# Sixty tiny matmuls at the head of the TensorE program, a reordered weight cast, a load in halves and an uneven last output

## The chip, the cores and the metric

The kernel runs on one core of one Trainium2 chip. The metric is the device time in microseconds (us). Each run also lists the core's span, which is 1.7 us shorter than its time in every run here (229.38 and 227.7 us in the first profile, for instance). Spans are used below where single executions are compared. A profile is the record of one such execution.

Engines: PE is TensorE, PEld its weight loads, DVE VectorE, ACT ScalarE, POOL GpSimd, SPq and ACTq the queues on which SyncE and ScalarE issue DMAs.

## The reference, cut to what matters

Linear attention with decay for 4 batches, 8 heads, 768 tokens of 64, followed by a gated feed-forward block (FFN) on 3072 tokens of 512:

```python
intra = einsum('bhic,bhjc->bhij', q, k) * Dmask      # per block, Dmask = lam ** (i - j), causal
inter = einsum('bhid,bhde->bhie', q * lam_pow, kv_state)
out   = einsum('bhij,bhjd->bhid', intra, v) + inter
kv_state = lam_block * kv_state + einsum('bhsd,bhse->bhde', k * rev_pow, v)
...
x = out as (3072, 512)
g = x @ w_gate
result = (g * sigmoid(g) * (x @ w_val)) @ w_out
```

Everything that decays comes from `lam`, eight numbers. They are spread over the partitions by one small matmul, the "lambda matmul" below.

## The kernel before

The kernel casts all inputs to bf16 and works on groups of 256 tokens. PE does everything in program order: attention of the first two groups, then FFN steps with the attention of later groups between them. Before its data arrives, PE is given filler matmuls whose results nobody reads:

```python
lam_ps = bank()
warm_up(4)                                   # four fillers of 512 columns (L130)
nc.tensor.matmul(lam_ps[:, 0:H], ones[:, 0:128], lam_row, ...)   # the lambda matmul (L163)
warm_up(3)
...
nc.scalar.activation(ln_lam, lam_ps[:, 0:H], AF.Ln)              # all decay tables follow (L175)
```

Further fillers stand between the attention matmuls of the first two groups (`warm_into`, L167). The plan of the FFN steps, where the change moves lines (steps between the lines shown are left out):

```python
at(s0[4], load_group, 2, "v")                # one DMA of 512 KB
at(s0[8], v_scale, 2, nc.gpsimd)             # v * decay for 8 heads in one instruction (L238)
...
at(s1b[3], cast_scaled, 5)                   # casts of group 5, then its DMA transpose (L251)
at(s1b[4], wo_cast)                          # output-weight casts (L232), 12 steps in six pieces
at(s1b[4], wo_cast)
at(s1b[6], wo_cast)
at(s1b[6], wo_cast)
at(s1b[6], v_scale, 5, nc.gpsimd)
at(s1b[8], wo_cast)                          # the fifth piece
at(s1b[10], wo_cast, ACTC)                   # the sixth, on ScalarE
at(s1b[11], ffn_out, 0, 0)                   # first output tile (L547): needs all six
at(s1b[11], ahead, 5)                        # group 5: update (L382: needs its v scale), scores (L326)
```

and the last output tile, which leaves in two parts:

```python
halves = ((0, DM // 2, nc.scalar.copy, nc.scalar), (DM // 2, DM, nc.vector.tensor_copy, nc.sync)) if last else ...
```

Of the kernel before, what the change touches and what calls it, by code (L numbers as in the profile page):

```python
# [19 lines left out]
@with_exitstack  # L20
def kernel(
    ctx: ExitStack,
    tc: tile.TileContext,
    q: bass.AP,
    k: bass.AP,
    v: bass.AP,
    lam: bass.AP,
    moe_w_gate: bass.AP,
    moe_w_val: bass.AP,
    moe_w_out: bass.AP,  # L30
    out: bass.AP,
):
    nc = tc.nc
    with tc.manual_schedule():
        _body(ctx, tc, nc, q, k, v, lam, moe_w_gate, moe_w_val, moe_w_out, out)


def _body(ctx, tc, nc, q, k, v, lam, moe_w_gate, moe_w_val, moe_w_out, out):
    B, H, S, D = q.shape
# [3 lines left out]
    DM = H * D  # L43
# [35 lines left out]
    def bank():  # L79
        b = banks[ring[0] % 8]  # L80
        ring[0] += 1
        return b
# [41 lines left out]
    warm = nc.const_aps.tensor(1.0, [128, 512], BF16)  # L124
    ones = const.tile([1, 128], FP32, name="ones")
    nc.vector.memset(ones, 1.0)
    def warm_up(n, cols=512):
        b = bank()
        for _ in range(n):
            nc.tensor.matmul(b[:, 0:cols], warm[:, 0:128], warm[:, 0:cols], start=True, stop=True)  # L130
# [28 lines left out]
           for b in range(B)]  # L159

    lam_ps = bank()
    warm_up(4)
    nc.tensor.matmul(lam_ps[:, 0:H], ones[:, 0:128], lam_row, start=True, stop=True)  # L163
    warm_up(3)
# [373 lines left out]
    def ffn_out(t, b, last=False):  # L538
        h_sb = st[("h", t)]
        osb = osb_pool.tile([128, DM], FP32, name="osb", tag="osb")  # L540
        row = groups[2 * t + b // 2][0] * S + (groups[2 * t + b // 2][1] * 2 + b % 2) * BLK
        halves = ((0, DM // 2, nc.scalar.copy, nc.scalar), (DM // 2, DM, nc.vector.tensor_copy, nc.sync)) \
            if last else ((0, DM, nc.scalar.copy, nc.scalar),)
        for c0, c1, fn, eng in halves:
            ps = bank()[:, 0:c1 - c0]
            for fc in range(FC):
                nc.tensor.matmul(ps, h_sb[:, fc, b], wo_sb[:, fc, c0:c1],  # L547
                                 start=(fc == 0), stop=(fc == FC - 1))
            fn(out=osb[:, c0:c1], in_=ps)  # L549
            eng.dma_start(out=bass.AP(tensor=out.tensor, offset=out.offset + row * DM + c0,  # L550
                                      ap=[[DM, 128], [1, c1 - c0]]),
                          in_=osb[:, c0:c1])
# [118 lines left out]
    def step(t, fc, b0=0, b1=B):  # L671
        steps.append((t, fc, b0, b1))
        return len(steps) - 1

    def at(n, fn, *a):
        plan.setdefault(n, []).append((fn, a))

    s0 = {fc: step(0, fc) for fc in range(2, FC - 1)}
# [5 lines left out]
    at(s0[3], swapped_q_table)  # L684
    at(s0[4], w_cast)
    at(s0[4], state, 1)
    at(s0[4], load_group, 2, "v")
    at(s0[5], load_group, 3)
    at(s0[6], w_cast)
    at(s0[7], load_group, 4, "kq")  # L690
# [2 lines left out]
    at(s0[8], pe_transpose, 2, 0)  # L693
    at(s0[8], pe_transpose, 2, 1)
    at(s0[8], w_cast)
    at(s0[8], v_scale, 2, nc.gpsimd)
    at(s0[9], scores, 2)
    at(s0[9], run_later, 4)
    at(s0[10], upd_mm, 2)
# [8 lines left out]
    s1b = [step(1, fc, 2, 4) for fc in range(FC)]  # L708
# [19 lines left out]
    at(s1b[6], run_later, 2)  # L728
    at(s1b[6], wo_cast)
    at(s1b[6], wo_cast)  # L730
    at(s1b[6], v_scale, 5, nc.gpsimd)
    at(s1b[8], wo_cast)
    at(s1b[9], core_a, 4)
    at(s1b[10], core_b, 4)
    at(s1b[10], wo_cast, ACTC)
    at(s1b[11], ffn_out, 0, 0)
    at(s1b[11], ahead, 5)
    at(s1b[11], run_later, 3)
    at(s1b[11], ffn_out, 0, 1)
    at(s1b[11], core_a, 5)  # L740
    at(s1b[11], ffn_out, 0, 2)
    at(s1b[11], core_b, 5)
    at(s1b[11], cast_scaled, 6)
# [62 lines left out]
```

## Time and profile before

| | before |
|---|---|
| median time | 228.14 us (227.94 to 228.56) |
| time of the profiled execution | 229.38 us, span 227.7 us |
| PE busy | 218.2 us, 96% of the span |
| PE idle between two equal fillers near 14.1 us | 0.62 us, released by "issue" |
| PE idle in the first output tile | 1.77 us, for a weight cast on POOL |

A timeline line reads: start, duration (with several instructions merged, from the first start to the last end), engine, line of the kernel, operation, output and inputs, count, and in brackets how long the engine had been idle and what released it. The lines that carry the argument stand in the prediction.

### The profile page before, as it was taken

What the parts mean: (1) busy time and instruction counts of PE and PEld (TensorE: products, weight loads), DVE (VectorE), ACT (ScalarE), POOL (GpSimd) and SP (SyncE); (2) the same over time, 40 slices, a digit from 0 to 9 for tenths busy, and PEclk for the clock granted to TensorE, in tenths of its full rate; (3) what the DMA queues carried; (4) which work ended last, traced back from release to release, by engine and by line L of the source; (5) the groups of instructions that cost most, each with busy time, mean ns of one, the idle gap of its engine ahead of it and who ended that gap; (6) DMA issues with size and microseconds to landing.
All of it is one profiled execution on the core that took longest, in us unless ns stands there. A gap on an engine that the chain in (4) does not pass through costs nothing.

```text
span 227.7 us, 5890 instructions
## 1 busy us (share of the span) xinstructions
PE 218.2 (96%) x2431; PEld 118.3 (52%) x2443; DVE 89.5 (39%) x151; ACT 107.2 (47%) x209; POOL 88.9 (39%) x131
## 2 busy tenths in 40 slices
PE   8789999999997999999999999999999999999994
PEld 3556456878853544454544544544544444444443
DVE  2664347685924213545362361353242123222200
ACT  5878585745562446464354363454433423322221
POOL 5676737641595232978373092092160000000000
PEclk9999999999999999999999999999999999999999
DMA  6999999899997879799877748815101101101122
GB/s 201 345 359 382 366 330 325 206 240 285 389 191 179 238 157 217 183 207 192 217 177 184 183 101 200 214 49 138 49 3 48 46 3 46 46 0 46 49 92 92
DMA packets 88012, 39.70 MB, mean 174 GB/s; under 512 B 57650, under 2 KB 83506, under 8 KB 87986
## 3 DMA queue, kind: packets, MB, share of 16 engines
q1 hardware_dynamic: 83474, 32.64, 55.3%
q10 hardware_dynamic: 4512, 6.69, 8.3%
q8 instruction: 19, 0.31, 0.6%
q14 instruction: 7, 0.06, 0.1%
HBM read 28.31 MB, written 6.29 MB: 152 GB/s over the span
## 4 chain that ended last, share of the span: by engine, by line
PE 82%; DMA 5%; SPq 5%; POOL 5%; issue 1%; ACT 0%; DVE 0%; DVEq 0%; POOLq 0%
PE bank L547 26%; PE bank L514 25%; PE bank L528 24%; SPq L99 4%; DMA woraw<-in_moe_w_out_dram 3%; DMA v<-in_v_dram 2%; POOL wo_sb L232 2%; POOL v_s L238 2%; PE bank L474 2%; PE bank L461 2%; PE bank L382 1%; PE bank L352 1%; SPq L227 1%; POOL kvf L421 1%; PE bank L326 0%
## 5 line engine op out<-in xcount | busy, mean ns | idle before, releaser
L531 DVE TENSOR_TENSOR h<-sil,bank 128x512 bf16<-128x512 bf16 (+1 forms) x87 | 51.5, 595 | 108.9 <-PE bank L528 93.2
L514 PE MATMUL bank<-xt,wg_sb 128*128 128x512 bf16 (+1 forms) x348 | 76.6, 343 | 0.0
L528 PE MATMUL bank<-xt,wv_sb 128*128 128x512 bf16 (+1 forms) x348 | 76.4, 342 | 0.0
L547 PE MATMUL bank<-wo_sb,h 128*128 128x512 bf16 (+1 forms) x288 | 64.3, 370 | 2.5 <-POOL wo_sb L232 1.8
L518 ACT ACTIVATE sil<-bank 128x512 bf16<-128x512 f32 (+1 forms) x87 | 45.8, 527 | 44.2 <-PE bank L514 41.2
L528 PEld LDWEIGHTS <-wv_sb 128*128 128x128 bf16 x348 | 34.0, 98 | 28.3
L547 PEld LDWEIGHTS <-h 128*128 128x128 bf16 x300 | 29.1, 98 | 34.3 <-issue 2.0
L514 PEld LDWEIGHTS <-wg_sb 128*128 128x128 bf16 x348 | 32.4, 98 | 27.2 <-DVE xt L486 0.3
L549 ACT COPY osb<-bank 128x512 f32<-128x512 f32 (+1 forms) x24 | 13.9, 578 | 55.4 <-PE bank L547 53.3
L238 POOL TENSOR_TENSOR v_s<-v,dec 128x1024 bf16<-128x1024 f32 (+1 forms) x14 | 23.2, 1667 | 14.4 <-DMA v<-in_v_dram 11.4
L421 POOL TENSOR_TENSOR kvf<-kvs,ups 128x256 f32<-128x256 f32 x8 | 5.8, 727 | 43.5 <-ACT ups L404 42.2
L333 DVE TENSOR_TENSOR ssb<-bank,causal 128x512 bf16<-128x512 f32 x24 | 15.3, 684 | 4.2 <-PE bank L326 4.1
L486 ACT CAST xt<-bank 128x512 bf16<-128x512 f32 x21 | 12.7, 663 | 2.9 <-PE bank L474 2.4
L421 POOL TENSOR_TENSOR kvf<-kvf,ups 128x256 f32<-128x256 f32 x16 | 13.4, 840 | 0.6
L430 POOL CAST kvn<-kvf 64x256 bf16<-64x256 f32 x24 | 11.6, 483 | 1.5
L404 ACT COPY ups<-bank 128x256 f32<-128x256 f32 (+1 forms) x24 | 9.5, 449 | 2.4 <-PE bank L382 1.4
L260 DVE TENSOR_TENSOR qk<-qraw,qdn 128x1024 bf16<-128x1024 f32 x6 | 7.7, 1280 | 4.5 <-DMA qraw<-in_q_dram 4.5
L258 ACT CAST qk<-kraw 128x1024 bf16<-128x1024 f32 x9 | 9.4, 1043 | 0.0
L357 DVE TENSOR_TENSOR ssb<-bank,causaln 128x512 bf16<-128x512 f32 x12 | 8.3, 688 | 1.2 <-PE bank L352 1.1
L232 POOL CAST wo_sb<-woraw 128x1024 bf16<-128x1024 f32 x5 | 5.1, 1040 | 7.3 <-DMA woraw<-in_moe_w_out_dram 7.3
L221 POOL CAST wv_sb<-wraw 128x1024 bf16<-128x1024 f32 (+1 forms) x6 | 5.8, 971 | 5.3 <-DMA wraw<-in_moe_w_val_dram 5.2
L474 PE MATMUL bank<-ssb,v_s 64*64 64x128 bf16 (+1 forms) x384 | 6.9, 208 | 0.5 <-ACT guard L445 0.5
(63 smaller groups left out, 117.2 us busy)
## 6 DMA issues: line engine op xcount, KB each, us to landing
out_dram<-osb ACTq DMA_DIRECT2D x23, 256.0 KB, 2.1
v<-in_v_dram SPq DMA_DIRECT2D x16, 256.0 KB, 4.7
woraw<-in_moe_w_out_dram SPq DMA_DIRECT2D x6, 512.0 KB, 7.4
kraw<-in_k_dram SPq DMA_DIRECT2D x24, 128.0 KB, 3.3
qraw<-in_q_dram SPq DMA_DIRECT2D x24, 128.0 KB, 3.6
wraw<-in_moe_w_gate_dram SPq DMA_DIRECT2D x5, 512.0 KB, 6.8
wraw<-in_moe_w_val_dram SPq DMA_DIRECT2D x5, 512.0 KB, 6.7
kraw<-in_k_dram SPq DMA_DIRECT2D x4, 512.0 KB, 6.9
```

The lines of the kernel that those rows point to most:

```text
L238: eng.tensor_tensor(out=st[("vs", g)][:, h0:h1], in0=st[("v", g)][:, h0:h1].rearrange("p h (s d) -> p h s d", s=2), in1=vfac(g, h0, h1), o ...
L333: nc.vector.tensor_tensor(out=ssb[:, h2, 2 * c:2 * c + 2].rearrange("p a s n -> p a (s n)"), in0=sp[(c, h2)].rearrange("p (a x) -> p a x", ...
L421: nc.gpsimd.tensor_tensor(out=o, in0=f, in1=u, op=ALU.add)
L430: nc.gpsimd.tensor_copy(out=o[64 - h2 * 64:128 - h2 * 64], in_=f[h2 * 64:h2 * 64 + 64])
L474: nc.tensor.matmul(op[r][h2 * 64:h2 * 64 + 64, cols(g, hp, s)], v_s[ps, 2 * hp + h2, s], ssb[ps, h2, hp * 2 + s] if g >= NAT0 else ssb[ps, ...
L486: fns[r](out=xt[:, g % 2, :, r].rearrange("p h (m s) -> p h s m", s=2) if g < NAT0 else xt[:, g % 2, :, :, r * M:r * M + M], in_=op[r].rea ...
L514: nc.tensor.matmul(gp[:, 0:N], wg_sb[:, mc, fs], xt[:, b0 // 2:b1 // 2, mc].rearrange("p g b n -> p g (b n)"), start=(mc == 0), stop=(mc = ...
L518: nc.scalar.activation(sil[:, 0:N], gp[:, 0:N], AF.Silu)
L528: nc.tensor.matmul(vp[:, 0:N], wv_sb[:, mc, fs], xt[:, b0 // 2:b1 // 2, mc].rearrange("p g b n -> p g (b n)"), start=(mc == 0), stop=(mc = ...
L531: nc.vector.tensor_tensor(out=h_sb[:, fc, b0:b1].rearrange("p b n -> p (b n)"), in0=sil[:, 0:N], in1=vp[:, 0:N], op=ALU.mult)
L547: nc.tensor.matmul(ps, h_sb[:, fc, b], wo_sb[:, fc, c0:c1], start=(fc == 0), stop=(fc == FC - 1))
L549: fn(out=osb[:, c0:c1], in_=ps)
```

## The change

The intent is to close the idle times of PE: the tiny matmuls put 120 PE instructions (60 matmuls and their weight loads) ahead of the 0.62 us hole (and cost little, it is hoped), on my guess that the hole stands at a fixed count of instructions, the cast is taken out from behind the v scale, group 2's v is scaled as its halves land, and the last copy and DMA get smaller.

The page's row `q8 instruction: 19, 0.31, 0.6%` is that of the instruction queue: 19 packets, each of 16,384 bytes in the traces of before. The expectations below call what one such packet carries a "block" and the packet its "fetch"; the "hole" is the idle time of 0.62 us near 14.1 us.

```diff
     lam_ps = bank()
+    b = bank()
+    for n in range(60):
+        r = slice(n % 2 * 64, n % 2 * 64 + 64)
+        nc.tensor.matmul(b[r, 0:8], warm[r, 0:64], warm[r, 0:8], start=True, stop=True, skip_group_check=True)
     warm_up(4)
...
-        halves = ((0, DM // 2, nc.scalar.copy, nc.scalar), (DM // 2, DM, nc.vector.tensor_copy, nc.sync)) \
+        halves = ((0, DM - 128, nc.scalar.copy, nc.scalar), (DM - 128, DM, nc.vector.tensor_copy, nc.sync)) \
...
-    at(s0[4], load_group, 2, "v")
+    at(s0[4], load_fp32, 2, nc.sync, v, "v", 0, H // 2)
+    at(s0[4], load_fp32, 2, nc.sync, v, "v", H // 2, H)
...
-    at(s0[8], v_scale, 2, nc.gpsimd)
+    at(s0[8], v_scale, 2, nc.gpsimd, 0, H // 2)
+    at(s0[8], v_scale, 2, nc.gpsimd, H // 2, H)
...
-    at(s1b[6], v_scale, 5, nc.gpsimd)
     at(s1b[8], wo_cast)
+    at(s1b[8], v_scale, 5, nc.gpsimd)
```

## The prediction

> **What bounds the kernel now.** I read the page first, then the chain of work that ended last, then the timeline of every engine in four stretches: the start, 26 to 40 us, 59 to 72 us and the last 5 us.
>
> ```profile
> PE 218.2 (96%) x2431; PEld 118.3 (52%) x2443; DVE 89.5 (39%) x151; ACT 107.2 (47%) x209; POOL 88.9 (39%) x131
> PE 82%; DMA 5%; SPq 5%; POOL 5%; issue 1%; ACT 0%; DVE 0%; DVEq 0%; POOLq 0%
> q8 instruction: 19, 0.31, 0.6%
> ```
>
> PE is busy for 96% of the span and carries 82% of the chain. From about 15 us on PE works almost without a break, so a microsecond is gained or lost only where PE waits, before PE gets going, or after its last matmul. The timeline of PE shows two waits above 0.6 us once its data has begun to arrive. They are these, with what stands around them:
>
> ```profile
> 13.83 0.28 PE L167 MATMUL bank<-const-bfloat16-1.0 128*128 128x256 bf16 x1
> 14.74 0.27 PE L167 MATMUL bank<-const-bfloat16-1.0 128*128 128x256 bf16 x1 [0.62 <-issue]
> ...
> 66.13 1.67 PE L547 MATMUL bank<-wo_sb,h 128*128 128x512 bf16 x7
> 66.62 1.91 POOL L238 TENSOR_TENSOR v_s<-v,dec 128x1024 bf16<-128x1024 f32 x1
> 68.48 1.03 POOL L232 CAST wo_sb<-woraw 128x1024 bf16<-128x1024 f32 x1
> 69.57 1.02 PE L547 MATMUL bank<-wo_sb,h 128*128 128x512 bf16 x4 [1.77 <-POOL wo_sb L232]
> 70.52 0.45 PE L382 MATMUL bank<-v_s,qk 64*64 64x64 bf16 x32
> ```
>
> In the first pair the two L167 matmuls are the two filler matmuls of one call: same operands, same bank, no semaphore between them. Nothing in the program can hold the second one back, yet it starts 0.91 us after the first. I read this as PE having run out of instructions. Counting the records in the trace, some 450 PE instructions had run by then[...].
>
> In the second group PE stands 1.77 us in the first output tile: its ninth contraction step needs the fifth output-weight cast, and GpSimd does group 5's v scale (1.91 us) before that cast.
>
> The start and the end:
>
> ```profile
> 0.84 1.86 PE L130 MATMUL bank<-const-bfloat16-1.0 128*128 128x512 bf16 x4 [0.84 <-PEq L790]
> 2.64 0.59 PE L163 MATMUL bank<-lam_row,ones 1*128 1x8 f32 x2
> 3.27 0.18 ACT L175 ACTIVATE ln_lam<-bank 128x8 f32<-128x8 f32 x1
> ...
> 224.36 0.42 DVE L549 COPY osb<-bank 128x256 f32<-128x256 f32 x1 [9.69 <-DMA out_dram<-osb]
> 224.82 0.38 SPq L550 DMA_DIRECT2D out_dram<-osb  x1
> ```
>
> The lambda matmul L163 follows directly on the four fillers, and ScalarE's logarithm follows directly on L163. The whole decay-table work hangs on it.
>
> [...] the first L130 matmuls of 512 columns start 0.43 us apart, and later ones of the same width 0.216 us (0.86 us for four in the chain); the records change pace at 5.4 us.[...]
>
> **The change part by part.**
>
> *60 tiny matmuls.* Each loads 64x64 weights and moves 8 columns, alternating between two opposite quarters of the array. The nearest row is L382: 32 matmuls of 64x64 on four quarters take 0.44 us; the last lasts 0.19, so 0.25 us for eight in each quarter, 31 ns apart at full clock, some 62 ns at half clock.[...] I take 1.7. They stand ahead of L130, so L163 slips from 2.64 to about 4.3. ScalarE was ready earlier (its table load ends at 3.12), so the tables, and with them the key casts, slip by the same. What comes back: about 0.15 us because the first transposes now fall after the clock change, and 0.18 us where ScalarE waited at 8.33 for a key DMA. GpSimd's v scales are held by v landing (11.34 us for group 1) and do not slip. So the masks of group 1, which end at 14.45, end near 15.8: 1.35 us later.
>
> What it buys:[...] Without the hole, group 1's intra matmuls, which now end at 15.5, would have ended near 14.85 (last mask 14.45, then half of the 32 matmuls). So this end moves to 14.85 + 1.35 = 16.2, which is **+0.65 us**. If the tiny matmuls cost only 0.6 us, it would be 0.3 to 0.4 us gained instead.
>
> *Group 2's v in halves.* Before, v lands at 34.7, the scale runs 34.77 to 36.68, and L382 starts at 36.73, where PE would have been free at 36.6. With halves the first can run when its half has landed, after GpSimd's cast ends at 34.3, and the second ends near 36.2. The gain is **-0.1 us**; with PE 0.65 us late the wait disappears anyway. The extra DMA issue (0.7 us on the queue at 28.4) moves the same bytes.
>
> *The cast ahead of the v scale.* The cast now runs 66.66 to 67.70 on GpSimd; the sixth, on ScalarE, ends at 67.9. PE would go on at 67.76 rather than 69.57. But then its four remaining matmuls end at 68.6, and the next in PE's order is L382 of group 5, which needs the v scale, now 67.70 to 69.6. GpSimd's sum is the same 2.94 us; only the four matmuls of 0.216 us now lie beside it. L382 moves from 70.52 to about 69.67: **-0.85 us**, not 1.77.
>
> *Last output in 384 and 128.* PE's work stays equal: 12 x (162 + 55 ns) against 12 x 2 x 109 ns. VectorE's final copy falls from 0.42 us to about 0.29 (half the columns; fitted from 0.42 at 256 and 0.69 at 512 for its other copies), and the last DMA carries 64 KB rather than 128. ScalarE's part then lands at about the same time. **-0.15 us.**
>
> Sum: +0.65 - 0.1 - 0.85 - 0.15 = -0.45, so 227.7. The cost of the tiny matmuls is the least certain term and I think it lies rather below than above what I worked out[...]; half the difference goes to the centre: **227.4 us**.
>
> **The rivals.**
> (1) The start decides: the tiny matmuls' time goes through to the end. For it: L163 and the logarithm have no slack. Against it: PE had spare time in fillers.[...]
> (2) The tiny matmuls are nearly free and the hole at 14.1 vanishes: about 226.5. Against more: the weight casts ffn needs end at 19.25 on ScalarE and 20.04 on GpSimd, 0.15 to 0.3 us before PE takes them, so a large part of an early gain runs into these DMAs.
> (3) The hole only moves[...]: it comes back near 12 or at 19 us, and the time is 228.0 to 228.3.
> (4) The whole 1.77 us at 69.57 is gained. Against: L382 needs the v scale; a new wait of about 1 us must appear there.
>
> **Range and chances.** The terms after 60 us are read from durations and are good to 0.2 us; the start is good to about 0.7. The range is 226.4 to 228.5. A move of 2% is 4.6 us, more than all waits in PE's timeline after its first data, so I give 1% to each side and 98% to within 2%.
>
> **What would show it.** L163 near 4.3 us and the logarithm behind it show the tiny matmuls' cost; at 3.2 the cost is small. The hole between two equal fillers should be gone. The first FFN gate matmul (L514, 15.51 before) tells the balance of the start: near 16.1 if I am right, below 15.3 under rival 2. The wait at the ninth step of the first output tile should go and L382 after it should wait about 1 us for the v scale. The time from PE's last matmul to the end should be 0.1 to 0.2 us shorter.[...]

The sum came to +0.65 - 0.1 - 0.85 - 0.15 = -0.45 us, so 227.7, less 0.3 us to 227.4. No term is gone as a whole, but parts of the first are: the 1.7 us in it is my estimate, a little below the 1.9 us that thirty times 62 ns give. With 1.9 the same working has +0.85 for the start and 227.9 for the sum. That the hole would go, and the 0.3 us taken off, were my estimates too.

"Half clock" there is a pace read from the trace, as the sentence on the first L130 matmuls says: 0.43 us for 512 columns at first, 0.216 us later. The trace's first clock record in this profile, a granted share of 1.00, begins at 5.46 us.

## The result, and the profile after

The changed kernel took 228.63 us in the median (228.37 to 229.22, five runs), where before took 228.14: a ratio of 1.002, with a 95% interval of 1.000 to 1.004. Ratios are the mean time of one kernel's fast runs over that of the other's in the same rounds, so not quite the ratio of the medians. The prediction of 227.4, with a range of 226.4 to 228.5, missed it by 0.13 us at the upper end, and the sign of its 0.7 us was not borne out.

In two later batches the changed kernel's medians were 228.43 and 228.13, with ratios to before of 0.9996 (0.9959 to 1.0033) and 0.9985 (0.9950 to 1.0019). All in all the change is worth nothing that these runs can tell from zero.

The profile of the changed kernel, from the page:

```profile
PE 219.4 (97%) x2490; PEld 119.6 (53%) x2503; DVE 89.2 (39%) x151; ACT 107.1 (47%) x209; POOL 89.0 (39%) x132
PE 89%; DMA 5%; ACT 2%; DVE 1%; issue 1%; DVEq 0%; ACTq 0%
```

Lines moved (those named here by 4: L163 is now L167, L547 is L551, L382 is L386, L326 is L330, L167 is L171, L514 is L518). The start in its timeline:

```profile
0.84 1.76 PE L165 MATMUL bank<-const-bfloat16-1.0 64*64 64x8 bf16 x60 [0.84 <-PEq L796]
4.36 0.59 PE L167 MATMUL bank<-lam_row,ones 1*128 1x8 f32 x2
4.99 0.18 ACT L179 ACTIVATE ln_lam<-bank 128x8 f32<-128x8 f32 x1 [1.87 <-PE bank L167]
...
14.93 0.39 PE L171 MATMUL bank<-const-bfloat16-1.0 128*128 128x256 bf16 x2
15.25 1.01 PE L478 MATMUL bank<-ssb,v_s 64*64 64x128 bf16 x32
16.20 0.61 PE L518 MATMUL bank<-xt,wg_sb 128*128 128x256 bf16 x4
```

The tiny matmuls take 1.76 us, and the lambda matmul slips from 2.64 to 4.36 us. ScalarE now idles 1.87 us for it. The two equal fillers are one merged row: the hole is gone. All the same the first FFN gate matmul starts at 16.20 us, where before has it at 15.51:

```profile
15.51 0.61 PE L514 MATMUL bank<-xt,wg_sb 128*128 128x256 bf16 x4
```

PE keeps nearly this distance up to the output tile (66.75 against 66.13).

The first output tile and group 5, and the tail:

```profile
64.05 3.02 POOL L236 CAST wo_sb<-woraw 128x1024 bf16<-128x1024 f32 x3
66.75 2.54 PE L551 MATMUL bank<-wo_sb,h 128*128 128x512 bf16 x11
67.03 1.92 POOL L242 TENSOR_TENSOR v_s<-v,dec 128x1024 bf16<-128x1024 f32 x1
69.22 0.50 PE L386 MATMUL bank<-v_s,qk 64*64 64x64 bf16 x32
70.36 0.64 PE L330 MATMUL bank<-qkt 64*64 64x128 bf16 x32 [0.64 <-DMA qkt<-qk]
...
224.00 0.29 DVE L553 COPY osb<-bank 128x128 f32<-128x128 f32 x1 [9.69 <-DMA out_dram<-osb]
```

The output tile runs through in one piece. PE does not wait for the v scale, which had ended at 68.95; instead the scores that follow wait 0.64 us for group 5's transposed keys and queries. The last copy is down from 0.42 to 0.29 us. From its start to the end of the span it is 3.07 us, where before it was 3.30.

So the two profiles show 227.7 and 227.1 us of span, which looks like a gain of 0.6 us, while the timed medians show a loss of 0.5. The two first profiles cannot both be usual executions. That was the first thing to test.

### The profile page after: what moved, and what is told of

Read it like the earlier page. It is cut to its first block, busy times and chain, and to the rows that moved or that the text cites. A ratio compares the mean times of both kernels' runs of the same rounds, so it can differ in the third digit from the quotient of the medians.

```text
span 227.1 us, 6010 instructions
## 1 busy us (share of the span) xinstructions
PE 219.4 (97%) x2490; PEld 119.6 (53%) x2503; DVE 89.2 (39%) x151; ACT 107.1 (47%) x209; POOL 89.0 (39%) x132
## 4 chain that ended last, share of the span: by engine, by line
PE 89%; DMA 5%; ACT 2%; DVE 1%; issue 1%; DVEq 0%; ACTq 0%
PE bank L518 27%; PE bank L532 26%; PE bank L551 26%; DMA qkt<-qk 5%; PE bank L478 2%; PE bank L465 2%; PE bank L386 1%; DVE ssb L337 1%; PE bank L330 1%; PE bank L293 1%; PE bank L356 1%; PE bank L165 1%; ACT qdec L187 1%; ACT qk L277 1%; PE bank L130 1%
## 5 line engine op out<-in xcount | busy, mean ns | idle before, releaser
L518 PE MATMUL bank<-xt,wg_sb 128*128 128x512 bf16 (+1 forms) x348 | 76.6, 343 | 0.0
L551 PE MATMUL bank<-wo_sb,h 128*128 128x512 bf16 (+2 forms) x288 | 64.2, 370 | 0.7 <-issue 0.2
L518 PEld LDWEIGHTS <-wg_sb 128*128 128x128 bf16 x348 | 32.4, 98 | 27.2 <-DVE xt L490 0.3
L551 PEld LDWEIGHTS <-h 128*128 128x128 bf16 x300 | 28.7, 98 | 32.9
```

Of the source, the lines that this page charges most:

```text
L518: nc.tensor.matmul(gp[:, 0:N], wg_sb[:, mc, fs], xt[:, b0 // 2:b1 // 2, mc].rearrange("p g b n -> p g (b n)"), start=(mc == 0), stop=(mc = ...
L551: nc.tensor.matmul(ps, h_sb[:, fc, b], wo_sb[:, fc, c0:c1], start=(fc == 0), stop=(fc == FC - 1))
```

## The experiments

Fifteen runs of eleven kernels were made, in four batches, each with runs of before on the same chip. All gave correct results.

### First batch: before again, and the parts one by one

**Before, unchanged.**

> The unchanged kernel once more, with its own profile and five rounds. Theory A (the first profile of before fell in an execution longer than the usual one: it took 229.38 us where the median is 228.14, so about 1.2 us of waits in it are not in the usual execution): the ratio is 1.000, the span of the new profile is about 226.5 us, and the wait of the first output tile for the fifth weight cast is well under the 1.77 us of the first profile, or the 0.6 us instruction hole is missing. Theory B (the profile is typical, the change gave back its gain elsewhere): span 227.5 or more, wait 1.5 us or more, hole 0.5 us or more.

Measured: 228.63 us in the median, ratio 0.998 (0.992 to 1.004). Its six spans were 226.1, 226.2, 226.4, 227.5, 227.7 and 228.4, and the profile fell on the longest. In that profile the wait of the output tile was 1.76 us, the hole 0.63. This does not decide, since the profile is of a long execution again. But it shows that one and the same kernel has executions 2.3 us apart, all at a mean granted clock of 0.998 to 1.000.

**Only the tiny matmuls** (the first hunk of the diff alone).

> Only the 60 tiny matmuls are added. My prediction's term: +0.65 us (first FFN gate matmul near 16.2 us as in the changed kernel's profile) and no hole between the two equal fillers. Theory A: +0.4 to +0.8 us in the timed runs, 228.6 to 228.9. Theory B: the tiny matmuls are not the loss, within 0.2 us of before.

Measured: 229.04 us against 228.17 (+0.87); the lowest span is 227.0 where before has 226.1. The first gate matmul is at 16.21 us, and there is no hole. The ratio of means is 1.0005 (0.996 to 1.005), as two of before's ten fast runs in this batch took over 230 us (an eleventh run was slow and is left out), so the timed runs alone do not show the loss. Median and lowest span agree with each other, a little above theory A's +0.4 to +0.8, and its form in the profile is exact. In this profile PE reaches the output tile at 66.76 us, waits there 0.77 us for the fifth cast, and L386 starts at 70.15.

**Everything but the tiny matmuls.**

```diff
-    b = bank()
-    for n in range(60):
-        r = slice(n % 2 * 64, n % 2 * 64 + 64)
-        nc.tensor.matmul(b[r, 0:8], warm[r, 0:64], warm[r, 0:8], start=True, stop=True, skip_group_check=True)
```

> The changed kernel without the 60 tiny matmuls. If the terms of the prediction for the other three parts hold in usual executions, 227.0 to 227.2 us (-1.0 to -1.1). Theory A: the cast and v scale order is worth less than 0.85 us in usual executions, so 227.7 to 228.0 (-0.2 to -0.4). Theory B: 227.0 or below.

Measured: 227.88 us (-0.29), lowest spans 225.4, 225.5 and 225.5. The profile (span 226.8) shows a wait of 0.42 us for the v scale, which the prediction had foreseen, and 0.72 us for the transposed keys:

```profile
69.01 0.45 PE L382 MATMUL bank<-v_s,qk 64*64 64x64 bf16 x32 [0.42 <-POOL v_s L238]
70.18 0.64 PE L326 MATMUL bank<-qkt 64*64 64x128 bf16 x32 [0.72 <-DMA qkt<-qk]
```

**Only the order of cast and v scale** (the last hunk alone).

> Only the order of the weight cast and group 5's v scale is changed. The prediction's term: -0.85 us, 227.3. Theory A: -0.3 us or less, since in a usual execution the weight's DMA lands so that the wait at the ninth step is shorter, and the wait for group 5's transposed keys and queries (0.64 us in the changed kernel) takes its place. Theory B: -0.6 to -0.9.

Measured: 228.15 us against 228.17 in the median; ratio 0.996 (0.991 to 1.001); lowest span 225.6 against 226.1, so -0.5 between the fastest executions. The profile fell on one of these (225.7). No wait of over 0.2 us is left between 60 and 76 us; L382 starts at 68.54.

### Two more profiles of before: what the wait is in a usual execution

**Before in the next batch.**

> The kernel before for a profile of a usual execution. Theory A: if its span is 226.2 to 226.5, the wait at the ninth step of the first output tile is 0.4 to 0.8 us, not 1.77, as the output weights land earlier and GpSimd's casts begin near 57.7 us; the instruction hole of about 0.6 us is there in any case. Theory B: wait 1.5 us or more in this too.

Measured: 229.18 us, ratio 1.0025 (0.997 to 1.008); spans from 226.0 to 229.1. The profiled execution had a span of 227.0, a wait of 1.03 us and a hole of 0.67.

**Before in the third batch.**

> The kernel before, for a profile of one of its usual executions (span 226.0 to 226.6). Then the wait at the ninth step of the first output tile should be 0.3 to 0.7 us (1.77, 1.76 and 1.03 in the profiles with spans 227.7, 228.4 and 227.0). If it is 1 us or more at such a span, the longer executions have another cause.

Measured: ratio 1.000 (0.997 to 1.003). This profile fell on a usual execution, with a span of 226.4:

```profile
57.03 1.04 POOL L232 CAST wo_sb<-woraw 128x1024 bf16<-128x1024 f32 x1 [4.68 <-DMA woraw<-in_moe_w_out_dram]
58.30 1.75 POOL L232 CAST wo_sb<-woraw 128x1024 bf16<-128x1024 f32 x1 [0.23 <-DMA woraw<-in_moe_w_out_dram]
...
65.31 1.91 POOL L238 TENSOR_TENSOR v_s<-v,dec 128x1024 bf16<-128x1024 f32 x1
66.16 1.67 PE L547 MATMUL bank<-wo_sb,h 128*128 128x512 bf16 x7
67.16 1.04 POOL L232 CAST wo_sb<-woraw 128x1024 bf16<-128x1024 f32 x1
68.25 1.02 PE L547 MATMUL bank<-wo_sb,h 128*128 128x512 bf16 x4 [0.41 <-POOL wo_sb L232]
69.20 0.45 PE L382 MATMUL bank<-v_s,qk 64*64 64x64 bf16 x32
```

Compare this with the lines in the prediction, and with these two of the same first profile:

```profile
59.41 1.04 POOL L232 CAST wo_sb<-woraw 128x1024 bf16<-128x1024 f32 x1 [7.09 <-DMA woraw<-in_moe_w_out_dram]
60.66 1.04 POOL L232 CAST wo_sb<-woraw 128x1024 bf16<-128x1024 f32 x1 [0.20 <-DMA woraw<-in_moe_w_out_dram]
```

PE comes to the output tile at the same moment (66.16 and 66.13 us). But POOL's v scale starts at 65.31 instead of 66.62, since its weight casts began earlier: the first at 57.03 instead of 59.41, the second at 58.30 instead of 60.66. Both wait for their DMA in both profiles. PE's wait is therefore 0.41 us, not 1.77. The four profiles of before line up:

| span of the profiled execution | second weight cast starts | wait in the output tile | L382 starts | from L382 to the end |
|---|---|---|---|---|
| 226.4 | 58.30 | 0.41 | 69.20 | 157.15 |
| 227.0 | 60.02 | 1.03 | 69.88 | 157.16 |
| 227.7 (the first profile) | 60.66 | 1.77 | 70.52 | 157.14 |
| 228.4 | 61.32 | 1.76 | 71.17 | 157.18 |

The last column is the end of the trace less the start of L382. It is constant to 0.04 us, so these four executions differ only ahead of L382, by when the output weights land and (in the last row) by 0.5 us at the start: there PE's clock changes only at 9.5 us (16 score matmuls take 0.62 us at 9.02, and 0.42 at 8.25 in the first profile), and the first gate matmul comes at 16.00. Theory A holds. Why the weights land later in some executions is not settled. The traces show that their first issue starts at 51.05 us in the usual execution and at 51.68 to 52.31 in the others, behind an issue of group 5's v that takes 1.99 us there and 2.56 to 2.77 in the others. A packet of the instruction queue runs beside that issue, for 1.26 us there and 1.74 to 2.35 in the others. So the packets treated below may have a part in this too; no run tests it.

### The delay and the shift of the program taken apart

**Tiny matmuls in place of the four fillers.** This keeps the shift of the program and takes the delay away.

```diff
-    warm_up(4)
     nc.tensor.matmul(lam_ps[:, 0:H], ones[:, 0:128], lam_row, start=True, stop=True)
```

> The changed kernel with the four 512-column fillers ahead of the lambda matmul left out, so that the 60 tiny matmuls stand in their place. If the loss is the delay of the lambda matmul: it starts near 2.6 us as in before, the hole between the two equal fillers stays away, the first FFN gate matmul is at 15.0 us or earlier (16.2 in the changed kernel), and the timed runs are 0.7 to 1.3 us below the changed kernel, near 227.0 to 227.5. Rival: the tiny matmuls themselves do harm (the clock change comes later, or the block of instructions is fetched late elsewhere); then the first gate matmul stays at 15.5 or later and the time is within 0.3 us of the changed kernel.

Measured: 228.32 us, against 228.43 for the changed kernel in this batch. The lambda matmul was at 2.53 us and the hole stayed away, as expected. But the first gate matmul was at 16.14 us: my theory failed, the rival's number held. The timeline says what happened:

```profile
9.19 0.69 SPq L216 DMA_DIRECT2D wraw<-in_moe_w_val_dram  x1
9.93 2.08 SPq L216 DMA_DIRECT2D wraw<-in_moe_w_gate_dram  x1
12.06 0.66 SPq L216 DMA_DIRECT2D wraw<-in_moe_w_val_dram  x1
12.22 0.61 POOL L276 CAST qk<-qraw 128x512 bf16<-128x512 f32 x1 [1.74 <-DMA qraw<-in_q_dram]
12.89 0.40 PE L292 MATMUL bank<-ident,qk 128*128 128x128 bf16 x4 [0.72 <-POOL qk L276]
```

From 8.46 us to 14.87 the load queue issues one DMA about every 0.7 us (0.65 to 0.69 each), except for one that takes 2.08 us. Group 1's second q half lands late, GpSimd waits 1.74 us for it, and the transposes and scores wait in turn. Before has such a long issue too, at 12.20 us, when q and v of group 1 have landed; the changed kernel has it at 10.74 us:

```profile
12.20 1.82 SPq L213 DMA_DIRECT2D wraw<-in_moe_w_val_dram  x1
```

```profile
10.74 1.66 SPq L217 DMA_DIRECT2D wraw<-in_moe_w_val_dram  x1
13.21 1.05 POOL L242 TENSOR_TENSOR v_s<-v,dec 128x512 bf16<-128x512 f32 x1 [0.68 <-DMA v<-in_v_dram]
```

The trace's packet records show the first packet of the instruction queue (16 KB, lasting some 0.95 us) starting at 12.3 us in before, 10.6 in the changed kernel and 10.1 here. The long issue goes with it: in all profiles the two start within 0.45 us of each other. My reading is that the packet goes with a hold-up of the loads behind it, of about a microsecond (the long issue takes 1.82 us in before, 1.66 in the changed kernel and 2.08 here, where the issues just before it take 0.69). That one causes the other is not shown, and a long issue is no sure sign of a packet: in every profile the load queue has one of 1.35 to 1.45 us near 3.9 us, with no instruction packet beside it. Moved earlier, it no longer comes after group 1's q and v have landed, but before. Here PE also waits 0.31 us for a weight cast at 21.57 us, and reaches the output tile only at 67.31. In this run PE's clock also changed late (8.3 us in the trace's clock records, 5.5 in the first profile of before; 16 score matmuls take 0.64 us at 6.53 here, 0.42 at 6.40 there). An unchanged kernel had it at 9.5 us in one profile and 4.2 in another, so I don't ascribe it to the tiny matmuls; but it may have its part in the 16.14.

**The changed kernel again.**

> The changed kernel once more, on the chip of this batch. Theory A (tiny matmuls +0.7, cast order -0.6, tail -0.2 in the fast executions): lowest span near 226.2 to 226.7. If the delay at the start also makes the wait for group 5's transposed keys regular: all spans 226.6 or more and a wait of 0.5 us or more for it in the profile.

Measured: 228.43 us, ratio 0.9996 (0.996 to 1.003). Spans 226.3 to 227.7; the profile fell on the lowest. It is the pair to the usual execution of before (226.4):

```profile
66.79 2.54 PE L551 MATMUL bank<-wo_sb,h 128*128 128x512 bf16 x11
67.24 1.91 POOL L242 TENSOR_TENSOR v_s<-v,dec 128x1024 bf16<-128x1024 f32 x1
69.25 0.45 PE L386 MATMUL bank<-v_s,qk 64*64 64x64 bf16 x32
69.53 0.62 PE L330 MATMUL bank<-qkt 64*64 64x128 bf16 x32
```

PE reaches the output tile 0.63 us later than before (66.79, 66.16), needs 2.46 us instead of 3.04 to L382 (69.25 - 66.79, 69.20 - 66.16), and ends 0.14 us sooner after it (157.01, 157.15). The sum is 0.63 - 0.58 - 0.14 = -0.09 us: no gain. The pair is not equal in everything: the weight casts begin at 59.04 us here and at 57.03 there. The profile with the tiny matmuls alone has them at 59.02, and PE at the output tile at 66.76, as here. Against it, L386 starts 0.90 us sooner here (69.25, 70.15). So what the order of cast and v scale is worth depends on when the weights land.

**Without the tiny matmuls again.**

> The change without the tiny matmuls once more, for a second profile and more rounds: lowest spans 225.4 to 225.5 again, a cluster there and a few runs 1 to 3 us longer. If its profile falls into a fast execution, the weight casts on GpSimd begin by 57.7 us and there is no wait for group 5's v scale or transposed keys of over 0.2 us.

Measured: 227.77 us, ratio 0.996 (0.992 to 1.000), spans 225.4 to 226.7. The profile (225.8) has the first weight cast at 57.82 us and neither of the two waits.

**Four more fillers instead of the tiny matmuls.** This keeps the delay and takes the shift away.

```diff
-    warm_up(4)
+    warm_up(8)
```

> The changed kernel with four more 512-column fillers in place of the 60 tiny matmuls: the same 1.7 us ahead of the lambda matmul, but 4 more matmuls instead of 60. It tells the delay from the shift of the instruction blocks. If the block shift is what takes the hole away: the hole of about 0.6 us is back, the block is fetched at about 12.5 us or later, the first FFN gate matmul is at 16.5 to 17.0 us (16.2 in the changed kernel), and the lowest spans are 0.3 to 0.6 us above those of the changed kernel. If the hole has gone for another reason, the first gate matmul is at 16.2.

Measured: 228.20 us, ratio 0.997 (0.995 to 1.000), spans 226.3 to 226.8. The lambda matmul is as late as in the changed kernel (the logarithm starts at 4.98 us, there at 4.99). The hole is back, but smaller:

```profile
15.40 0.22 PE L382 MATMUL bank<-v_s,qk 64*64 64x64 bf16 x3 [0.41 <-issue]
...
16.45 0.61 PE L514 MATMUL bank<-xt,wg_sb 128*128 128x256 bf16 x4
```

I had expected 16.5 to 17.0 us and a loss of time. The loss did not come. With the same delay, the shift of the program by 60 tiny matmuls is worth 0.25 us at the first gate matmul (16.45 less 16.20) and nothing in the timed runs. The delay alone is seen against the version without tiny matmuls, from which this kernel differs by four fillers: the first gate matmul is at 16.45 us against 15.49 and 15.76 there, and the lowest span is 226.3 against 225.4. By the ratios to before (0.997 here, 0.997 and 0.996 there) the delay cannot be told from nothing. So the delay is a cost that the profiles and the fastest executions show, and what it buys is small.

**Thirty tiny matmuls in place of two fillers.**

```diff
-    for n in range(60):
+    for n in range(30):
...
-    warm_up(4)
+    warm_up(2)
```

> The changed kernel with 30 tiny matmuls in place of the first two fillers, so that the lambda matmul stays near 2.6 us and the block boundary moves half as far. Theory (the block's fetch holds up the load queue for over 1 us wherever it falls): the one long issue on the load queue (2.0 us at 9.9 us with 60 in place of four, 1.7 at 10.7 in the changed kernel, 2.0 at 12.1 without) is at 10.6 to 11.5 us, the second half of group 1's v lands late, near 13.2 us, and the first gate matmul is at 15.2 to 15.7. Rival (the late q and v of the kernel with 60 for four fillers were chance): no long issue before 12 us, first gate matmul at 15.0 or earlier.

Measured: 229.19 us, ratio 1.0015 (0.999 to 1.004), spans 226.8 to 227.9. The long issue (2.10 us) sits at 11.44 us, as expected, and the packet at 11.8. They came together again; that the one causes the other is not shown by this either. The miss: v still landed in time, with the v scale at 12.40. The first gate matmul came at 15.39 us, only 0.12 ahead of before, and even that was lost at once:

```profile
14.15 0.41 PE L386 MATMUL bank<-v_s,qk 64*64 64x64 bf16 x27 [0.31 <-issue]
15.39 0.61 PE L518 MATMUL bank<-xt,wg_sb 128*128 128x256 bf16 x4
...
19.77 1.04 POOL L225 CAST wv_sb<-wraw 128x1024 bf16<-128x1024 f32 x1 [2.61 <-DMA wraw<-in_moe_w_val_dram]
20.87 0.82 PE L532 MATMUL bank<-xt,wv_sb 128*128 128x512 bf16 x3 [0.48 <-POOL wv_sb L225]
```

Here a weight cast waits 2.61 us for its DMA and starts at 19.77 us (19.00 in before), and PE waits 0.48 us for it. I know no place for this packet without a wait beside it.

**Fewer instructions instead of more.** The version without tiny matmuls also loses the eight small fillers between 9 and 15 us.

```diff
-    warm_into(up[0], 1)                      # twice
-    warm_into(st[("op", 0)][0], 1)           # twice
-    warm_into(st[("op", 1)][0], 2)
-    pe_transpose(1, 1, (0, 1), warm=1)
+    pe_transpose(1, 1, (0, 1))
```

> The version without tiny matmuls, and without the eight small fillers between 9 and 15 us.[...] first gate matmul at 15.2 to 15.35 us (15.5 without), 0.15 to 0.3 us faster than without tiny matmuls, lowest span near 225.2. Rival: PE's clock falls or comes late, and it is slower.

Measured: 227.32 us against 228.59, ratio 0.996 (0.992 to 1.000), spans 225.2, 225.4, 225.6, 225.6, 227.4 and 227.9. The hole is 0.45 us, now within the attention matmuls. In all eleven profiles that have a hole it stands after 449 PE records (in the first profile of before 223 weight loads, 222 matmuls and 4 of PE's sequencer), whichever instruction comes next: with eight fillers fewer, with four more, and with thirty tiny matmuls for two fillers. So its place goes with the count of instructions. The first gate matmul is at 14.98 us, better than expected. It is the lowest median of all, though the interval touches 1 and two long executions are among the six.

### Is it the wait for the transposed keys?

The first profile of the changed kernel had 157.85 us from L386 to the end, 0.84 more than the 157.01 of its usual execution, with the 0.64 us wait in it.

```diff
-    at(s1b[3], cast_scaled, 5)
+    at(s1b[1], cast_scaled, 5)
```

> The changed kernel with group 5's scaled casts, and so its transpose, two FFN steps (1.7 us) earlier. If the wait for the transposed keys is what holds the changed kernel's usual executions: no such wait, all spans within 226.0 to 226.6, 0.3 us or more below e14 in the median. Rival (the transpose shares the transfers with the output weights and ends when they end, or holds these up): the transpose is issued near 57.5 us but lands no earlier, or GpSimd's weight casts begin later, and the median is within 0.2 us of e14 or above it.

Measured: 228.48 us, spans 226.6 to 228.0. There is no wait for the transposed keys, but the weight casts begin at 59.52 us (58.48 in the profile of the run below), and L386 waits 0.34 us for the v scale. That is what the rival had said: the transpose and the output weights share the transfers, and what one gains the other loses. But it is one profile, and the casts of the unchanged kernel begin anywhere from 57.03 to 60.07 us, so it is not shown.

> The changed kernel again, as the comparison of this batch: spans 226.3 to 227.7, median 226.6 to 226.9, and about 0 to +0.3 us against before.

Measured: 228.13 us, spans 226.1 to 227.8, ratio 0.9985 (0.995 to 1.002): by median 0.35 us below the version with the earlier cast. Its profile (226.1) has no such wait. So the wait belongs to some executions of the changed kernel, as of others, and is not what holds it back as a rule.

> The version without tiny matmuls and without the small fillers, with the same earlier cast: lowest spans 225.1 to 225.3 as without it (225.2); if the wait for the transposed keys is what makes its longer executions (227.4, 227.9), these go and the median falls below 225.6. Rival: the spread stays as it was.

Measured: 227.97 us, spans 225.2 to 228.4. The spread stayed as it was; the earlier cast is no improvement here either.

## Why the prediction was wrong

Two steps failed: 0.3 us were taken off the sum without a ground, and the cast term of -0.85 us was priced from a long execution (-0.58 in the usual pair). The terms were also added up as if each stood alone.

**What bounds it: right.** PE carried 89% of the chain after the change, and every gain or loss sat at one of the places named.

**The tiny matmuls: right in the delay and its size.** I put 1.7 us for them, and they took 1.76 (59 ns for each of the 30 in a quarter, where 62 had been worked out from L382). I put the lambda matmul near 4.3 us, and it was at 4.36. I put the balance of the start at +0.65 (my own figures, 16.2 less 15.5, give 0.7), and it was +0.69 (16.20 less 15.51) and still +0.63 at the output tile. The hole went as foreseen. That the inner terms were right as well is not shown: the clock change, which I took from one profile (5.4 us; four transposes take 0.63 us ahead of it there and 0.40 at 9.00), came at 4.2, 5.5, 7.5 and 9.5 us in the four of before, and at 6.6 in the changed kernel's first. Then I wrote that the cost "lies rather below than above what I worked out" and took 0.3 us off the sum. Nothing in the profile supported that, and it was the first wrong step.

**The cast ahead of the v scale: the term that was mis-sized.** "L382 moves from 70.52 to about 69.67: -0.85 us" was read from an execution in which the wait was 1.77 us, and then subtracted from a median of executions in which it is mostly far shorter. In the usual pair of executions the way from the output tile to L382 shortened by 0.58 us (3.04 to 2.46). The new wait for the v scale, about 1 us in my working, was 0.29 to 0.42 us in three profiles and absent in the others, as the weight casts start earlier there than in the profile I read, or PE comes later. In the run with the earlier cast of keys and queries they start as late (the second at 60.75 us, 60.66), PE comes 0.64 us later, and the wait is 0.34. Equally, in the two first profiles the same way shortened by 1.92 us (4.39 to 2.47), of which 0.64 came back at the transposed keys. The size of this term is a matter of the execution.

**The sum: two terms that are not independent.** I added the start's +0.65 to the cast's -0.85. But a PE that comes later to the output tile waits less there. With the tiny matmuls alone PE came 0.63 us later than in the first profile of before and the fifth cast started 0.37 us sooner (68.11, 68.48); the wait was 0.77 us, which is 1.77 less 0.63 and 0.37. In my own working L382 was set by GpSimd's v scale at 69.6, so the late start would have been absorbed there. In the usual execution of the changed kernel PE waits for neither cast nor v scale, and the late start counts.

**The halves of v: not shown. The tail: right.** L382 of group 2 started at 36.66 instead of 36.73 us without the tiny matmuls, but it started at 36.68 in the run with only the cast order changed, which has no halves. The tail is 0.23 us shorter by the first two profiles (3.30 to 3.07 us); I had said 0.15.

**The rivals.** Rival 1, that the start decides, is nearest to what happened. Rival 3 was half right: the hole did not come back in the changed kernel, but a long issue stood on the load queue beside the packet wherever it was put (at 9.93, 10.74, 11.44, 12.20 and 13.40 us in five kernels, 1.42 to 2.10 us long), which I had not thought of. Rival 2's limit, the weight casts that leave little slack, showed itself in the run with thirty tiny matmuls.

**The sum with the measured terms** of the usual pair is 228.14 + 0.63 - 0.58 - 0.14 = 228.05 us. The three medians of the changed kernel were 228.63, 228.43 and 228.13 (the last two lie inside my range) while those of before lay between 228.14 and 229.0 by batch. Over all batches the medians are 228.62 us for before (61 fast runs), 228.41 for the changed kernel (17), 227.77 without the tiny matmuls (12) and 229.04 with them alone (6): the parts nearly cancel. The rest is within the scatter of the executions: before's spans go from 226.0 to 229.3 us over 61 fast runs, the changed kernel's from 226.1 to 227.8 over 17. I had set a range of +-1 us around a centre that was too low, and had not counted this scatter. Why an execution is long, beyond the late output weights, is not settled; three of before's longest (228.5, 228.6 and 229.3 us) also had a lower mean clock than the rest, 0.990 to 0.993.

## What to carry to other kernels

Compare the profiled execution's own time with the median before a wait in it is used as a budget; here the difference of 1.2 us was more than the 0.7 us that the plan hoped to win. Price what stands ahead of a chain's first link in full: PE had idle time and fillers, but the lambda matmul had no slack, so 1.76 us of "free" work made the first gate matmul 0.69 us late and the output tile 0.63. Where PE stands between two instructions that nothing in the program holds apart (0.52 to 0.67 us in the four profiles of before) and the place goes with the count of instructions, try fewer instructions before padding: with 60 tiny matmuls more the hole went, but the long issue only moved (from 12.20 to 10.74 us); that this is faster is not shown (227.32 us with eight fillers fewer, 227.77 without that cut).
